# Attention in pairs of units and a values product of eight rounds, in a kernel of attention and two MLPs on one Trainium2 core

## The chip, the cores and the metric

The kernel runs on one core of one Trainium2 chip. The metric is device time in microseconds (us), the median of several executions. The engines are named as in the profile: PE (TensorE matmuls) and PEld (its weight loads), DVE (VectorE), ACT (ScalarE), POOL (GpSimd), SP (SyncE, which issues all the transfers here).

## The reference: what is computed

Attention with windows over 4 batches, 8 heads, 576 positions and 64 dimensions, then two MLPs on its 2304 x 512 output, all in float32:

```python
rel = pos[:, None] - pos[None, :]
mask_plain = (rel >= 0) & (rel < window)                                   # window 32, heads 0 to 3
mask_dil = (rel >= 0) & (rel < window * dilation) & (rel % dilation == 0)  # dilation 4, heads 4 to 7
scores = np.where(masks[None], scale * q @ k.T, -1e9)
attn = np.exp(scores - scores.max(-1)) ; attn = attn / (attn.sum(-1) + 1e-09)
x = (attn @ v)                       # as (2304, 512)
h = x @ w_in;  x = (h * sigmoid(1.702 * h)) @ w_out         # first MLP, 512 -> 2048 -> 512
h = x @ w_in2; y = relu(h) ** 2 @ w_out2                    # second MLP
```

## The kernel before

**Attention.** The dilated heads are reordered by the host so that both kinds of mask become a band: a query looks at its own block of 32 keys and the one before. A *unit* is one batch, one pair of heads and one half of the positions (288): 32 units in all, 8 a batch. For a unit `attend` (L488) loads q and k as one tile `qk` and three pieces of `v` (L497, L503), makes the scores of three blocks of 96 queries in 18 small matmuls on tiles of 64 rows by 32 columns of the array (`scores`, L517), adds the mask and takes the maximum on DVE (`maxima`, L530), exponentiates with a sum on ACT (`exps`, L537), adds 1e-9 and takes the reciprocal on DVE (L551, L554), normalises on POOL, ACT or DVE (L562), transposes in blocks of 32 on DVE (L575) and multiplies by v (`values`, L589). The values product goes block of queries by block: for each 32 queries, once with the keys before and once with their own keys, on three row groups and two column groups, 36 matmuls in all. Every matmul of float32 leaves two records in the trace, so a scores product shows as x36 and a values product as x72. Each is one round after another over the six array tiles. The results in PSUM are cast to a high part and a low part of x (L284 or L286 and L605).

**The MLPs.** They work on high and low parts, three matmuls for one product. The first MLP goes over five blocks of columns of x (`BLOCKS1`) and in each over 16 slices f of the hidden layer: `hidden` (L639 to L641, 12 matmuls), tanh on ACT, products on DVE, and `project` (L694 to L696, 12 matmuls). Its weights come as 64-bit words by L350 into three `raw` buffers, are put together by ACT or DVE (`raw_top`), DVE (`raw_join`, L361) and split into `wp` tiles, one for each two slices. The second MLP (from L1088) is by Strassen-like products. Attention of batch 0 comes first, ahead of the first block; the units of batches 1 to 3 are put in between the matmuls of blocks 0 to 2.

**The order.** `Schedule` (L100) is a planner that runs while the program is built: each task has a cost on its engine, a wanted time, the tasks it comes after and the buffers it takes, and the planner fixes the order of each engine from them. The constants at the head of the file (T_START, SCORES, SPACE and so on) are its costs and due times. While PE has nothing to do in the start, it puts warming matmuls on zeros in (L770). At run time every engine and SP's queue take their work in that order.

**Buffers.** Two `qk` and two `v`, three `sm`, two `pt` for every batch, so the load for a unit waits until a unit two earlier has been used. In PSUM there are three pairs of banks ("pr"; a unit's scores take one, its values one) and two single banks ("h"), of which the values of a unit take one and the hidden layer the others.

Of the kernel before, what the change touches and what calls it, by code (L numbers as in the profile page):

```python
# [7 lines left out]
F32 = mybir.dt.float32  # L8
# [28 lines left out]
T_START = 25.81  # L37
T_ATT = 2.38
A0 = 0.29
A1 = 0.82  # L40
SM_BUFS = 3
SCORES, VALUES = 0.74, 0.76
MAXIMUM, EXP = 0.13, 0.33

AHEAD = (47, 38, 43)
# [6 lines left out]
PREP = 9.31  # L52
# [3 lines left out]
RAW_FROM = 7.67  # L56
WARM = 256
WARM_FOR = 5
MASK_AT = -9.0
MASK_MORE = 10.0  # L60
LEAD = (23.0, 2, 5.33)
SPACE = 2.8
# [3 lines left out]
SPARE_POOL = (0.38, 2.22, 3.74)  # L66
SPARE_ACT = (0.54, 0, 0)
SPARE_TO = (33.64, 233.24)
# [10 lines left out]
UNITS = (8, 8, 8)  # L79
# [15 lines left out]
X_EARLY = 14.7  # L95
X_FROM = 3.48
X_WANT = 6.8
# [141 lines left out]
def attention_mlp_mlp(  # L239
# [27 lines left out]
    mask_sb = att.tile([QB, 5, P], BF16, name="mask_sb")  # L267
    mask_band = att.tile([QB, 5, 2 * WIN], BF16, name="mask_band")

    places = {  # L270
        "pr": 3, "o": 0, "h": 2, "s": 0, "c": C_BUFS, "qk": 2, "v": 2, "sm": SM_BUFS, "st": 3, "pt": 2,
# [150 lines left out]
    def x_pieces(b, p, u):  # L422
# [4 lines left out]
        per = size // NBLK  # L427
        jobs = []
        for n, blk in enumerate(BLOCKS1):
            width = sum(e - a for _, _, a, e in blk)  # L430
            runs, col = [], 0
            for bb, r, a, e in blk:
                if bb == b:
                    if plain:
                        lo, hi = max(a, size * u), min(e, size * (u + 1))
                        if lo < hi:
                            runs.append((r, lo - size * u, hi - size * u, col + lo - a))
                    elif r // 2 == u:
                        runs.append((0, (r % 2) * ROW + a, (r % 2) * ROW + e, col))
                col += e - a  # L440
# [3 lines left out]
            for r, lo, hi, c in runs:  # L444
                while lo < hi:
                    k = lo // per
                    end = min(hi, per * (2 if k == 0 and lo == 0 and hi >= 2 * per else k + 1))
                    cuts.append((r, lo, end, c))
                    c, lo = c + end - lo, end
            while cuts:  # L450
                r, lo, hi, c = cuts.pop(0)
                rows = 1
                inset = (lo + size * u) % ROW
# [9 lines left out]
                def src(m, r=r, rows=rows, lo=lo - k * per, hi=hi - k * per, k=k, both=both):  # L463
                    o = m["ab"][:, :, 0:QB] if both else m["c"][:, 0:QB] if k == 2 else m["ab"][:, k, 0:QB]
# [23 lines left out]
    def attend(b, p, u, want, start, n0):  # L488

        m = {}  # L490
        kinds = ((1, 0, 0), (0, 0, 0))[u] if p < NPAIR // 2 else (2, 3, 4)
        src = qkv_in[b, p, u]
        qk_b, v_b, sm_b, st_b, pt_b, s_b, ab_b, c_b = (buffer(c) for c in ("qk", "v", "sm", "st", "pt", "pr", "pr", "h"))

        def load_qk():
            m["qk"] = qkv.tile([P, UQ + UK], F32, tag="qk", bufs=2, name="qk")
            nc.sync.dma_start(m["qk"], src[:, 0:UQ + UK])  # L497

        def load_v():
            m["v"] = qkv.tile([QB, NBLK + 1, P], F32, tag="v", bufs=2, name="v")  # L500
            for a in range(NBLK):
                at = UQ + UK + a * P
                nc.sync.dma_start(  # L503
                    m["v"][a * WIN:(a + 1) * WIN], src[:, at:at + P].rearrange("(t k) d -> k t d", t=NBLK + 1)
                )

        d_qk = task("dma", 0.87, want - 5, load_qk, (), [qk_b])
        d_v = task("dma", 0.65, want - 1, load_v, (), [v_b], count=3)

        def scores():  # L510
            m["s"] = bank_pair(s_b)
            for i in range(NBLK):
                for a in range(NBLK):
                    w = (NBLK * a + i) * WIN
                    for j in range(2):
                        js = slice(D * j, D * (j + 1))
                        T.matmul(  # L517
                            m["s"][a * WIN:(a + 1) * WIN, j, i * KW:(i + 1) * KW],
# [882 lines left out]
```

## Time and profile before

| what | value |
|---|---|
| median of 3 runs | 837.87 us (836.74 to 838.67) |
| the profiled execution, its own time | 835.73 us |
| its span, from the first to the last instruction | 834.0 us |
| PE busy / PEld busy | 821.1 us (98%) / 739.8 us (89%) |
| DVE / ACT / POOL busy | 570.9 (68%) / 411.8 (49%) / 10.7 us (1%) |
| mean granted clock of TensorE | 0.994 |
| DMA | 171.70 MB, 206 GB/s over the span |

The profile is of one execution, whose time is 1.7 us more than its span. Busy shares are means over the whole span; the rows below look into single stretches. A start in a timeline is in us from the start of the span, and the second number is how long the group of instructions lasted; ends of matmuls are modelled, so starts are the safer numbers.

### The profile page before, as it was taken

How to read it: one execution, taken by the hardware profiler on the slowest of the kernel's cores; microseconds unless marked ns; L12 is line 12 of the kernel's file. 1: busy time of each engine (PE TensorE's matmuls, PEld its weight loads, DVE VectorE, ACT ScalarE, POOL GpSimd, SP SyncE). 2: the span in 40 equal slices, each digit the busy share in tenths (PEclk: the TensorE clock that was granted, in tenths of full speed). 3: DMA queues.
4: the chain of work that ended last, by engine and by line, in shares of the span. 5: the costliest groups of instructions: out<-in, count | busy, mean ns of one | idle time of the engine just before them, and what ended most of it. 6: DMA issues, size and time to landing. Idle time of an engine off the chain costs nothing.

```text
span 834.0 us, 18713 instructions
## 1 busy us (share of the span) xinstructions
PE 821.1 (98%) x7480; PEld 739.8 (89%) x7480; DVE 570.9 (68%) x1443; ACT 411.8 (49%) x1052; POOL 10.7 (1%) x23
## 2 busy tenths in 40 slices
PE   6999999999999999999999999999999999999998
PEld 4787778777789998888888899999999999999998
DVE  3788887645446778887797646587855687655784
ACT  5777676343336544443454345534455435455432
POOL 2200000000000000000000000000000000000000
PEclk9799999999999999999999999999999999999999
DMA  6666655221113248888956770877777696767751
GB/s 204 166 182 222 188 195 186 87 51 51 42 57 94 61 130 283 287 283 284 331 191 246 262 312 1 302 297 243 278 295 260 239 375 209 274 243 272 286 206 58
DMA packets 64311, 171.70 MB, mean 206 GB/s; under 512 B 6016, under 2 KB 36320, under 8 KB 58848
## 3 DMA queue, kind: packets, MB, share of 16 engines
q1 hardware_dynamic: 64224, 170.50, 59.4%
q8 instruction: 59, 0.97, 0.5%
q14 instruction: 28, 0.23, 0.1%
HBM read 131.68 MB, written 38.80 MB: 204 GB/s over the span
## 4 chain that ended last, share of the span: by engine, by line
PE 98%; issue 1%; DMA 1%; DVE 0%; ACT 0%; SPq 0%
PE ps L639 9%; PE ps L694 9%; PE ps L640 8%; PE ps L641 8%; PE ps L695 8%; PE ps L696 8%; PE ps L1244 7%; PE ps L1088 7%; PE ps L1089 7%; PE ps L1243 7%; PE ps L1245 7%; PE ps L1090 7%; PE ps L589 4%; PE ps L517 2%; PE ps L770 1%
## 5 line engine op out<-in xcount | busy, mean ns | idle before, releaser
L639 PE MATMUL ps<-x,wp 128*128 128x512 f32 (+3 forms) x328 | 123.1, 375 | 0.0
L694 PE MATMUL ps<-gh,wp 128*128 128x512 f32 (+3 forms) x328 | 122.2, 373 | 0.0
L640 PE MATMUL ps<-x,wp 128*128 128x512 f32 (+3 forms) x328 | 120.5, 367 | 0.0
L641 PE MATMUL ps<-x,wp 128*128 128x512 f32 (+3 forms) x328 | 120.4, 367 | 0.0
L695 PE MATMUL ps<-gh,wp 128*128 128x512 f32 (+3 forms) x328 | 119.3, 364 | 0.0
L696 PE MATMUL ps<-gl,wp 128*128 128x512 f32 (+3 forms) x328 | 119.3, 364 | 0.0
L1245 PE MATMUL ps<-gl,ws 128*128 128x384 f32 x336 | 112.2, 334 | 0.0
L1243 PE MATMUL ps<-gh,ws 128*128 128x384 f32 x336 | 112.2, 334 | 0.0
L1244 PE MATMUL ps<-gh,ws 128*128 128x384 f32 x336 | 112.2, 334 | 0.0
L284 ACT CAST gh<-gq 128x768 fp32r<-128x768 f32 x84 | 68.5, 838 | 78.3 <-PE ps L1244 57.5
L295 DVE TENSOR_TENSOR gl<-gq,gh 128x768 fp32r<-128x768 f32 x84 | 80.4, 957 | 34.2 <-PE ps L1245 28.2
L666 ACT ACTIVATE g<-ps 128x512 f32<-128x512 f32 (+3 forms) x82 | 44.7, 545 | 94.3 <-PE ps L641 94.0
L1088 PE MATMUL ps<-xo,ws 128*128 128x384 f32 x252 | 84.2, 334 | 0.0
L1089 PE MATMUL ps<-xo,ws 128*128 128x384 f32 x252 | 84.2, 334 | 0.0
L1090 PE MATMUL ps<-xo,ws 128*128 128x384 f32 x252 | 84.2, 334 | 0.0
L537 ACT ACTIVATE sm<-sm,st 96x64 f32<-96x64 f32 x192 | 64.5, 341 | 22.7 <-DVE st L530 22.4
L669 DVE SCALAR_TENSOR_TENSOR g<-g,ps 128x512 f32<-128x512 f32 (+3 forms) x82 | 50.5, 616 | 35.0 <-ACT g L666 34.5
L639 PEld LDWEIGHTS ps<-x,wp 128*128 128x128 f32 x328 | 62.8, 192 | 11.0 <-ACT sm L537 0.2
L641 PEld LDWEIGHTS ps<-x,wp 128*128 128x128 f32 x328 | 62.9, 192 | 10.0
L694 PEld LDWEIGHTS ps<-gh,wp 128*128 128x128 f32 x328 | 61.7, 188 | 11.1
L640 PEld LDWEIGHTS ps<-x,wp 128*128 128x128 f32 x328 | 63.0, 192 | 9.0
L696 PEld LDWEIGHTS ps<-gl,wp 128*128 128x128 f32 x328 | 61.8, 188 | 10.1
(73 smaller groups left out, 1427.4 us busy)
## 6 DMA issues: line engine op xcount, KB each, us to landing
ws<-wo_s SPq DMA_DIRECT2D x42, 1024.0 KB, 7.1
raw<-in_w SPq DMA_DIRECT2D x64, 511.8 KB, 4.7
ws<-wi_s SPq DMA_DIRECT2D x36, 896.0 KB, 6.4
wo_s<-wt SPq DMA_DIRECT2D x16, 896.0 KB, 7.5
wi_s<-wt SPq DMA_DIRECT2D x16, 896.0 KB, 6.0
qk<-in_qkv SPq DMA_DIRECT2D x32, 304.0 KB, 3.2
v<-in_qkv SPq DMA_DIRECT2D x96, 64.0 KB, 2.6
xs<-x2d SPq DMA_DIRECT2D x12, 384.0 KB, 5.8
```

The source lines that it names most:

```text
L639: T.matmul(out, w_hi[:, ks], x[:, 0, k, a:z], start=(k == 0), stop=False)
L640: T.matmul(out, w_hi[:, ks], x[:, 1, k, a:z], start=False, stop=False)
L641: T.matmul(out, w_lo[:, ks], x[:, 0, k, a:z], start=False, stop=(k == KD - 1))
L694: T.matmul(out, w_hi[:, ds_], m["gh"], start=(f == 0 and a == 0), stop=False)
L695: T.matmul(out, w_lo[:, ds_], m["gh"], start=False, stop=False)
L696: T.matmul(out, w_hi[:, ds_], m["gl"], start=False, stop=(f == KF - 1))
L1088: T.matmul(out, wt[:, 0, a, ks], hi, start=(first and k == 0), stop=False, skip_group_check=True)
L1089: T.matmul(out, wt[:, 0, a, ks], lo, start=False, stop=False, skip_group_check=True)
L1090: T.matmul(out, wt[:, 1, a, ks], hi, start=False, stop=(k == 1), skip_group_check=True)
L1243: T.matmul(out, w[:, 0, j, ds_], hi, start=(first and j == 0), stop=False, skip_group_check=True)
L1244: T.matmul(out, w[:, 1, j, ds_], hi, start=False, stop=False, skip_group_check=True)
L1245: T.matmul(out, w[:, 0, j, ds_], lo, start=False, stop=(j == NPR - 1), skip_group_check=True)
```

## The change

Three things, and new numbers for the planner.

1. Outside batch 0, `attend` takes both units of a head pair at once (`us = (0, 1)`): one scores product of 36 matmuls, twelve maxima and exponentials, one guard, one reciprocal, two normalisations, one transpose of 768 columns and one values product. `sm` and `pt` are single buffers of double width, `st` has four. Batch 0 still goes unit by unit.
2. The values product goes by keys. Each 32 keys of v are loaded into the array once, for the 64 queries that look at them (32 at both ends): 24 matmuls for a unit in place of 36.
3. In batch 0 q, k, v, sm, pt and the uncut masks lie in the places of the weight tiles 5, 6 and 7 of the first MLP, which are not in use then, so that no unit shares a buffer with another for q, k and v.

```diff
-T_START = 25.81
-T_ATT = 2.38
+T_START = 25.47
+T_ATT = 1.94
...
-SM_BUFS = 3
-SCORES, VALUES = 0.74, 0.76
+SM_BUFS = 1
+SCORES, VALUES = (0.74, 1.1), (0.8, 1.28)
...
-UNITS = (8, 8, 8)
+UNITS = (4, 4, 4)
...
+    first = {f: wpool.tile([P, 4096], F32, tag=f"wp{f}", bufs=1, name="first") for f in (5, 6, 7)}
+    q_first = [first[7][:, n * (UQ + UK):(n + 1) * (UQ + UK)] for n in range(6)]
+    q_first += [first[5][:, n * (UQ + UK):(n + 1) * (UQ + UK)] for n in range(2)]
+    v_first = first[6][:QB].rearrange("k (n t d) -> k n t d", n=8, t=NBLK + 1)
...
-    def attend(b, p, u, want, start, n0):
+    def attend(b, p, us, want, n0):
...
+        def load_qk(k):
+            m["qk", k] = q_first[n0] if first else qkv.tile([P, UQ + UK], F32, tag="qk", bufs=2, name="qk")
+            nc.sync.dma_start(m["qk", k], qkv_in[b, p, us[k], :, 0:UQ + UK])
...
-        scored = task("pe", SCORES, want, scores, [d_qk] + maxima_of.get(n0 - 2, []) + moved_of.get(n0 - SM_BUFS, []), [qk_b, s_b])
+        gate = maxima_of.get(n0 - 2, []) + moved_of.get(n0 - (4 if first else SM_BUFS), [])
+        scored = task("pe", SCORES[n - 1], want, scores, d_qk + gate, qk_bs + [s_b])
...
         def values():
-            m["ab"], m["c"] = bank_pair(ab_b), bank(c_b)
-            for i in range(NBLK):
-                for e in range(2):
+            ab, c = bank_pair(ab_b), bank(c_b)
+            for k in range(n):
+                ks = slice(QB * k, QB * (k + 1))
...
+                for i in range(NBLK + 1):
+                    lo, hi = max(0, i - 1), min(NBLK, i + 1)
                     for a in range(NBLK):
                         rows = slice(a * WIN, (a + 1) * WIN)
+                        o = (ab[:, a] if a < 2 else c)[:, ks]
                         for j in range(2):
                             js = slice(D * j, D * (j + 1))
-                            o = m["ab"][js, a] if a < 2 else m["c"][js]
                             T.matmul(
-                                o[:, i * WIN:(i + 1) * WIN], m["v"][rows, i + e, js], m["pt"][rows, j, i, e],
-                                start=(e == 0), stop=(e == 1), tile_position=(a * WIN, D * j), skip_group_check=True,
+                                o[js, lo * WIN:hi * WIN], m["v", k][rows, i, js],
+                                m["pt"][rows, k, j, max(0, i * KW - WIN):min(NBLK * KW, i * KW + WIN)],
+                                start=(i == 0), stop=(i == NBLK), tile_position=(a * WIN, D * j), skip_group_check=True,
                             )
...
-        for i, (p, u) in enumerate(ORDER):
-            attend(b, p, u, wants[(b - 1) * nu + i], False, b * nu + i)
+        for p in range(NPAIR):
+            attend(b, p, (0, 1), wants[(b - 1) * NPAIR + p], nu + (b - 1) * NPAIR + p)
```

What moves is shown at three places. The first is PE, just ahead of the first dense matmuls of the first MLP. Before (L517 scores, L589 values, L639 to L641 hidden layer):

```order
L589 MATMUL ps<-pt,v 64x32 x36
L517 MATMUL ps<-qk 32x64 x18
L589 MATMUL ps<-pt,v 64x32 x36
L517 MATMUL ps<-qk 32x64 x18
L639 MATMUL ps<-x_311,wp 128x288
L640 MATMUL ps<-x_311,wp 128x288
L641 MATMUL ps<-x_311,wp 128x288
```

And with the change (L623 values, L675 to L677 hidden layer):

```order
L623 MATMUL ps<-first 64x32 x6
L623 MATMUL ps<-first 64x64 x12
L623 MATMUL ps<-first 64x32 x12
L623 MATMUL ps<-first 64x64 x12
L623 MATMUL ps<-first 64x32 x6
L675 MATMUL ps<-x_326,wp 128x288
L676 MATMUL ps<-x_326,wp 128x288
L677 MATMUL ps<-x_326,wp 128x288
```

Ahead of the first dense matmul there are now the values of two units in one go, 24 matmuls each, and no scores of batch 1 any more. In both programs six units' values stand ahead of it and two behind. Warming matmuls are 28 in place of 40.

The second place is SP's queue in the start (L497 and L503 load q with k and v; L350 the first MLP's weights; L732 and L733 the later masks). Before:

```order
L497 DMA qk<-in_qkv 128x608
L732 DMA mask_sb<-in_masks 96x256
L733 DMA mask_sb<-in_masks 32x64
L497 DMA qk<-in_qkv 128x608
L503 DMA v<-in_qkv 32x4x128 x6
L497 DMA qk<-in_qkv 128x608 x2
L350 DMA raw<-in_w 128x2047 x3
L497 DMA qk<-in_qkv 128x608
L503 DMA v<-in_qkv 32x4x128 x3
```

With the change (L514 and L520 load q with k and v, L770 and L771 the later masks, L362 the weights):

```order
L514 DMA first<-in_qkv 128x608 x2
L520 DMA first<-in_qkv 32x4x128 x3
L770 DMA first<-in_masks 96x256
L771 DMA first<-in_masks 32x64
L514 DMA first<-in_qkv 128x608
L520 DMA first<-in_qkv 32x4x128 x3
L514 DMA first<-in_qkv 128x608
L520 DMA first<-in_qkv 32x4x128 x9
L362 DMA raw<-in_w 128x2047 x4
L514 DMA qk<-in_qkv 128x608 x2
L520 DMA v<-in_qkv 32x4x128 x6
```

The first three weight loads moved from behind 14 other transfers to behind 36, all of batch 0's loads among them.

The third place is PE in the first block of the first MLP, around a values product. Before:

```order
L639 MATMUL ps<-x_311,wp 128x512
L640 MATMUL ps<-x_311,wp 128x512
L641 MATMUL ps<-x_311,wp 128x512
L589 MATMUL ps<-pt,v 64x32 x36
L694 MATMUL ps<-gh,wp 128x512
L695 MATMUL ps<-gh,wp 128x512
L696 MATMUL ps<-gl,wp 128x512
```

With the change:

```order
L731 MATMUL ps<-gh,wp 128x224
L732 MATMUL ps<-gl,wp 128x224
L623 MATMUL ps<-pt,v 64x32 x6
L623 MATMUL ps<-pt,v 64x64 x12
L623 MATMUL ps<-pt,v 64x32 x12
L623 MATMUL ps<-pt,v 64x64 x12
L623 MATMUL ps<-pt,v 64x32 x6
L730 MATMUL ps<-gh,wp 128x224
L731 MATMUL ps<-gh,wp 128x224
L732 MATMUL ps<-gl,wp 128x224
```

One product of 48 matmuls for two units stands where two of 36 stood at different places. Batches 1 to 3 have 12 such products and 12 scores products of 36 matmuls, where there were 24 and 24 before. The dense matmuls of both MLPs are as many as before.

## Rows read from the trace of the kernel before

**Rows 1.** The page: busy time of each engine; chain that ended last, by engine.
```profile
PE 821.1 (98%) x7480; PEld 739.8 (89%) x7480; DVE 570.9 (68%) x1443; ACT 411.8 (49%) x1052; POOL 10.7 (1%) x23
...
PE 98%; issue 1%; DMA 1%; DVE 0%; ACT 0%; SPq 0%
```

**Rows 2.** Waits of PE, whole span: us in total, times, longest us.
```profile
PE ps L517 <- DMA qk<-in_qkv: 3.6, 2, 2.2
PE ps L517 <- issue: 2.7, 1, 2.7
PE ps L589 <- issue: 1.3, 1, 1.3
...
PE ps L589 <- DVE pt L575: 0.6, 2, 0.3
```

**Rows 3.** Timeline of PE, 30.4 to 35.7 us: start, us, engine, line.
```profile
31.35 0.69 PE L589 MATMUL ps<-pt,v 32*64 32x32 f32 x44 [0.30 <-DVE pt L575]
33.36 0.85 PE L589 MATMUL ps<-pt,v 32*64 32x32 f32 x28 [1.32 <-issue]
34.15 0.88 PE L517 MATMUL ps<-qk 64*32 64x64 f32 x36
34.96 0.61 PE L639 MATMUL ps<-x,wp 128*128 128x288 f32 x1
```

**Rows 4.** The page, DMA queues: packets, MB, share of 16 engines.
```profile
q8 instruction: 59, 0.97, 0.5%
```

**Rows 5.** Groups of ACT, 6 to 35 us: count, busy and mean ns, idle before.
```profile
L537 ACT ACTIVATE sm<-sm,st 96x64 f32<-96x64 f32 x44 | 14.8, 347 | 7.3 <-DVE st L530 7.3
...
L284 ACT CAST x<-ps 128x24 fp32r<-128x24 f32 (+7 forms) x22 | 3.3, 238 | 4.8 <-PE ps L589 4.8
L284 ACT CAST wp<-raw 128x512 fp32r<-128x512 f32 x3 | 1.8, 680 | 0.0
L284 ACT CAST c<-raw 128x512 f16<-128x512 bf16 x2 | 1.5, 760 | 0.0
```

**Rows 6.** Timeline of PE around a scores product, 77.2 to 79 us.
```profile
77.27 0.39 PE L694 MATMUL ps<-gh,wp 128*128 128x512 f32 x1
...
77.72 0.39 PE L696 MATMUL ps<-gl,wp 128*128 128x512 f32 x1
78.04 0.62 PE L517 MATMUL ps<-qk 64*32 64x64 f32 x36
...
78.94 0.40 PE L695 MATMUL ps<-gh,wp 128*128 128x512 f32 x1
```

**Rows 7.** Timeline of PE around a values product, 87.6 to 89.5 us.
```profile
87.85 0.39 PE L641 MATMUL ps<-x,wp 128*128 128x512 f32 x1
88.17 0.98 PE L589 MATMUL ps<-pt,v 32*64 32x32 f32 x72
...
89.41 0.39 PE L640 MATMUL ps<-x,wp 128*128 128x512 f32 x1
```

**Rows 8.** Stretches: us; busy PE, PEld, DVE, ACT, POOL; granted clock; DMA share; GB/s.
```profile
34.96:44.00 9.04, 9.04 (x184) 8.30 (x181) 5.35 (x30) 5.23 (x28) 0.83 (x1) 0.53 0.81 228
60.00:120.00 60.00, 60.00 (x764) 47.69 (x753) 52.56 (x171) 42.22 (x131) 0.00 (x0) 1.00 0.64 203
```

**Rows 9.** Timeline of SP's queue: start, us, line, transfers issued.
```profile
3.53 2.80 SPq L503 DMA_DIRECT2D v<-in_qkv  x6
...
8.73 1.38 SPq L350 DMA_DIRECT2D raw<-in_w  x3
...
12.96 2.37 SPq L503 DMA_DIRECT2D v<-in_qkv  x3
```

**Rows 10.** Line L350 (weights into raw), 0 to 45 us: issue to landing.
```profile
DMA to landing us min/median/max: 4.0/5.5/8.0
```

**Rows 11.** Groups of DVE by form: the low parts of the first MLP's weights.
```profile
L295 DVE TENSOR_TENSOR wp<-raw,wp 128x512 fp32r<-128x512 f32 x32 | 21.4, 677 | 0.2
```

**Rows 12.** Timeline of ACT: its first exponential.
```profile
6.05 0.35 ACT L537 ACTIVATE sm<-sm,st 96x64 f32<-96x64 f32 x1 [4.04 <-DVE st L530]
```

More of the change, by code (lines that the diff above doesn't have):

```diff
@@ L427, in x_pieces @@
         per = size // NBLK
+        before = size * u
         jobs = []
@@ L510, in scores @@
+        since = 0.0 if first else NEXT_FROM
+        d_qk = [task("dma", 0.87, at_qk, lambda k=k: load_qk(k), (), [qk_bs[k]], since=since) for k in range(n)]
+        d_v = [task("dma", 0.65, at_v, lambda k=k: load_v(k), (), [v_bs[k]], count=3, since=since) for k in range(n)]
         def scores():
-            m["s"] = bank_pair(s_b)
-            for i in range(NBLK):
[L513 to L518, printed above, removed]
-                            m["qk"][js, w:w + WIN], m["qk"][js, UQ + w:UQ + w + KW],
-                            start=True, stop=True, tile_position=(D * j, a * WIN), skip_group_check=True,
-                        )
@@ L523, in attend @@
-        scored = task("pe", SCORES, want, scores, [d_qk] + maxima_of.get(n0 - 2, []) + moved_of.get(n0 - SM_BUFS, []), [qk_b, s_b])
-        def maxima(j, i):
+            m["s"] = bank_pair(s_b)[:, :, 0:n * NBLK * KW].rearrange("q j (u c) -> q u j c", u=n)
+            for k in range(n):
+                for i in range(NBLK):
+                    for a in range(NBLK):
+                        w = (NBLK * a + i) * WIN
+                        for j in range(2):
+                            js = slice(D * j, D * (j + 1))
+                            T.matmul(
+                                m["s"][a * WIN:(a + 1) * WIN, k, j, i * KW:(i + 1) * KW],
+                                m["qk", k][js, w:w + WIN], m["qk", k][js, UQ + w:UQ + w + KW],
+                                start=True, stop=True, tile_position=(D * j, a * WIN), skip_group_check=True,
+                            )
@@ L577, in attend @@
-        moved = task("dve", 0.5, want, turn, [t], [sm_b, pt_b])
+                    out=sm, in0=sm, op=ALU.mult,
+                    in1=m["st"][:, 2, k].rearrange("q j (i o) -> q (j i) o", o=1).to_broadcast([QB, 2 * NBLK, KW]),
+                )
+        t = task("dve", 0.1, want, guard, es, [st_b], True)
+        t = task("dve", 0.15, want, recip, [t], [st_b], True)
+        ways = {"pool": 0.84, "dve": 0.44} if first else {"act": 1.5, "dve": 0.44}
+        normal = [
+            task(tuple(ways), tuple(ways.values()), want, lambda e, k=k: normalise(e, k), [t], [st_b, sm_b] + own, True)
+            for k in range(n)
+        ]
@@ L578, in attend @@
+        def turn():
+            m["pt"] = pt_first[:, pt_b["id"]] if first else att.tile([QB, n, 2, NBLK * KW], F32, tag="pt", bufs=1, name="pt")
+            V.transpose(
+                out=m["pt"].rearrange("k u j c -> k (u j c)"), in_=m["sm"].rearrange("q u j i c -> q (u j i c)")
+            )
+        moved = task("dve", 0.07 + 0.38 * n, want, turn, normal, [sm_b, pt_b] + own)
         moved_of[n0] = [moved]
         def values():
-            m["ab"], m["c"] = bank_pair(ab_b), bank(c_b)
@@ L644, in step @@
             if f < 2 and k == 0:
-                before = before + [v for u in range(2) if z > FIRST or u == 0 for v in values_of[blk["i"], u]]
+                before = before + [v for u in range(2) if z > FIRST or u == 0 for v in values_of.get((blk["i"], u), [])]
             t = task(
@@ L725, in attention_mlp_mlp @@
     nu = len(ORDER)
+    first_b = {f: buffer(f"wp{f}") for f in (5, 6, 7)}
     def load_masks():
```

190 lines of the change are left out of this document (98 added, 92 removed).

## The prediction

> **What bounds the kernel now.** I first read the busy shares and the chain that ended last [rows 1]: TensorE is busy for 98% of the span and is itself 98% of the chain. So only two things can shorten the run: fewer microseconds of work on PE, or less waiting on it. Next I read the waits of PE over the whole span [rows 2]. Apart from 1.1 us for the zeros of the first warming matmul there are four entries, 8.2 us in all, and none of them comes after the first layer has begun: from the first L639 on, PE waits for nobody. The timeline of PE at that place [rows 3] gives the start of the first layer, 34.96 us. I therefore split the profiled execution (span 834.0 us, time 835.73 us) into a start of 34.96 us, limited by latencies, and 799 us in which PE sets the pace, and reckon the two apart.
>
> The start is worth a closer look. Two of its waits, 2.73 and 1.32 us, have "issue" as their releaser and lie in the middle of a product (44 records of a values product, then nothing, then the other 28) [rows 2, 3]. No tile is waited for there. Queue q8 brought 59 packets [rows 4] for 14,960 instructions of PE and its loads [rows 1], some 254 to a packet, so I read these gaps as PE waiting for its own code. The other waits are for q and k (3.6 us). In the same stretch ACT, which does the exponentials, sat idle 7.3 us for DVE and 4.8 us for PE [rows 5], so no engine was full.
>
> After the start the cost of attention on PE is what it pushes the dense matmuls apart. Around a scores product [rows 6] the dense matmuls before and two after start at 77.72 and 78.94, 1.22 us apart; two steps of a dense 512-column matmul take 0.454 us (77.27 to 77.72 is two steps, 0.227 each), so the scores push in 0.77 us. Around a values product [rows 7] it is 87.85 to 89.41, 1.56 less 0.454, so 1.11 us. A scores product has 36 records in 6 rounds over its six array tiles, a values product 72 in 12. If a round costs the same in both, 6 rounds are 0.34 us: **0.057 us a round and 0.43 us fixed** for breaking into the dense stream.
>
> **The change, part by part, after the start.** (1) Values with each 32 keys once: 8 rounds a unit where there were 12. (2) Two units together: one fixed part where there were two, for scores and for values. Before, two units cost 2 x (0.77 + 1.11) = 3.75 us. Now the scores take 0.43 + 12 x 0.057 = 1.11 us and the values 0.43 + 16 x 0.057 = 1.33 us, so 2.44 us. That is 1.30 us for each of the 12 pairs of batches 1 to 3, 15.7 us. Two corrections: one scores product of batch 1 stood ahead of the first L639 before (34.15 in [rows 3]) and stands behind it now, +0.8 us; the two units of batch 0 still left behind it save 0.23 us each, -0.5 us. Together **-15.3 us**.
>
> The one unknown price is a round of 64 weight columns and 64 moving columns. The scores round has 32 and 64, the values round 64 and 32, and the trace has none with both wide. If the wider operand alone counts, a round stays at 0.057 us. If the sum of columns counts (96 in both old forms, 128 now), it is 0.076 us, and 4 such rounds in each of 26 units cost 2.0 us. I take 0.057, since the nearest rows, both with a 64 in them, give it, and keep 13.3 us of gain as the other end. No row gives less than 0.057.
>
> (3) On the other engines the exponentials, maxima and pieces of x stay as many; guard, reciprocal and transposes become fewer and longer. All this lies beside PE and is costed at nothing. The work that hides it is the dense stream, and the thinnest cover is 60 to 120 us, where DVE is busy 52.56 of 60 us and PE still never waits [rows 8]. With two to three pairs at 1.30 us less in it, the same DVE work has to fit into some 57 us, and DVE is 92% full. I allow **+0.5 us** for small new waits; where the cover goes altogether is a rival.
>
> **The start.** Batch 0's q, k and v now have places of their own, so no load waits for a buffer, but the first weights are issued behind all 36 transfers of attention and masks instead of behind 14. SP issued six in 2.80 us [rows 9], 0.467 each, so the first raw starts at 0.73 + 36 x 0.467 = 17.5 us instead of 8.73. Its transfer takes 4.0, 5.5 or 8.0 us (least, middle, most) [rows 10], so it lies there at 23.0 us in the middle case. Then ACT makes the top part (0.76), four exponentials and two casts that stand in between (1.3 and 0.3), the high part (0.68), and DVE the low part (0.68) [rows 5, 11]: 3.7 us, so 26.7 us. The join lies beside the exponentials. The other path is ACT's own: from its first exponential (6.05 [rows 12], unchanged, since the first masks and the first unit's q and k are still the first three issues) 42 exponentials of 0.336 (14.8 us for 44), 18 casts of 0.15 (3.3 us for 22), top and high part, together 18.3 us, so 24.3 us if it never waits [rows 5]; in-order waits, such as POOL cutting the later masks ahead of the third unit's normalisation, bring it near the first path. Both end close together. I take 28.0 us for the first dense matmul, between the middle and the slow transfer, because SP's pitch grew to 0.79 us (2.37 for three) while the DMA engines were loaded [rows 9]. Ends: 25.2 us with the quickest transfer, 30.5 with the slowest and a hand-over more. **34.96 - 28.0 = -7.0 us.** PE's code waits may come again, but a stop of PE now costs less: the next units' loads no longer wait for PE to free a buffer, so ACT and DVE have work queued meanwhile.
>
> At the start of the first layer the granted clock was 0.53 on average from 34.96 to 44 us [rows 8], near its lower level of 1.2 GHz, after the second code wait. The change keeps a stretch of this kind: fewer warming matmuls (28 for 40) and products between the first dense steps. I cost the difference at nothing, with -3 us (high level at once) and +2 us (a longer stretch) as ends.
>
> **Sum.** -15.3 + 0.5 - 7.0 = -21.8 us against 835.73, so **814 us**. The profiled execution stands 2.1 us under the median of the runs, 837.87, so by the median it would be 816; the range takes both in.
>
> **The rivals.** (a) *The wide round costs its sum of columns.* For it: each tile must take 64 weight columns and 64 moving ones. Against it: the two old rounds cost the same with either operand wide. Time 816. A rule of the Trainium skill would bring it about (page "TensorE: Matmul & The Clock Gate", section "Part 3: Packing small matmuls — row/col tiling"): a weight load overlaps a running matmul only in another row group, and here two tiles share each row group. No run here shows it for 64 by 64. Chance 0.15, next to the forecast and inside its range.
>
> (b) *The first layer waits for the weights.* If SP keeps the loaded pitch of 0.79 us [rows 9] for all 36, the raw starts at 29.2, lands at 34.7 and the first dense matmul is at 38.4: the start loses 3.4 us and 835.73 - 14.8 + 3.4 = 824 us. Against it: 0.79 was seen with three large weight loads in flight, which now come last. Chance 0.08.
>
> (c) *DVE and ACT become the bound in the first block.* For it: 88% of DVE in [rows 8], and single buffers for a pair's sm and pt, so that the next pair's scores wait for this pair's transpose. If the 5.2 us that four pairs save in this block are all waited away, 819 us. Chance 0.12.
>
> (d) *The pair's values hold their PSUM banks too long*, which ends on the other side. A pair takes a bank of "h" until both units' casts and subtractions are done, and the hidden layer has only two such banks; PE would then wait at each of the 12 pairs. It decides from 22 / 12 = 1.8 us of wait a pair; at 2.5 us it gives 814 + 30 = 844. Against it: with one unit's hold PE waited not once behind the start [rows 2], and the order leaves dense products of the second kind behind most pairs. Chance 0.04. That the change does less than it says is hardly open: the order shows 24 matmuls for a unit's values in place of 36.
>
> **How the numbers follow.** Forecast (808 to 818) 0.61, (a) 0.15, (c) 0.12, (b) 0.08, (d) 0.04. The range goes from 807 us (high clock at once and a start at 25.2, with all of the gain) to 823 us (waits of (c), or a late start, by the median's measure). A difference of 0.2%, 1.7 us, is about what a measurement of this kernel tells from none. Only (d), and (b) with (c) together beyond what each costs, end above that: slower 0.04, same 0.02, faster 0.94.
>
> **What would show it.** Right: the first dense matmul near 28 us; a pair's values with 96 records pushing in 1.33 us and its scores 1.11 us; no PE wait behind the start. A push of 1.49 us for the values would be (a); PE waits on DVE or ACT between 40 and 120 us (c); a first dense matmul after 33 us (b). The sum is wrong if PE still waits for code for several microseconds at the start, or if the stretch at the lower clock lasts beyond 15 us.

## The result and the profile after

| what | before | with the change |
|---|---|---|
| median of the runs | 837.38 us (836.74 to 838.67, 4 runs) | 815.66 us (815.59 to 816.05, 4 runs) |
| the profiled execution, its span | 835.73, 834.0 us | 815.61, 813.8 us |
| first dense matmul of the first MLP | 34.96 us | 30.81 us |
| from there to the end of the span | 799.0 us | 783.0 us |

The ratio is 0.974, with an interval of 0.972 to 0.976. The forecast was 814 us and a range of 807 to 823, so the time and the sign were right. Of 20.2 us of span, 4.15 came from the start and 16.05 from the part behind it; the forecast had 7.0 and 14.8. So the start brought 2.85 us less than forecast and the part behind it 1.25 us more. That the two partly cancel is luck; the rest of this document is about them.

The page of the changed kernel (busy times; chain that ended last, by engine), beside [rows 1]:

```profile
PE 800.2 (98%) x6700; PEld 727.0 (89%) x6700; DVE 556.1 (68%) x1380; ACT 420.2 (52%) x1074; POOL 10.3 (1%) x23
...
PE 96%; DMA 2%; SPq 1%; DVE 1%; ACT 0%; issue 0%
```

PE is still the bound, with 780 matmul records fewer (7480 to 6700). Its waits over the whole span (us in total, times, longest), beside [rows 2]:

```profile
PE ps L538 <- DMA first<-in_qkv: 4.5, 4, 2.1
PE ps L538 <- issue: 2.0, 2, 1.6
PE ps L623 <- DVE first L604: 1.8, 1, 1.8
...
PE ps L675 <- DVE x L641: 0.5, 1, 0.5
```

Only the last entry lies behind the start (it comes at 255.7 us). The stretch of the first block and that after the first dense matmul (columns as in [rows 8]):

```profile
34.96:44.00 9.04, 8.95 (x171) 8.35 (x172) 8.75 (x45) 7.14 (x27) 0.24 (x1) 1.00 0.85 276
60.00:120.00 60.00, 60.00 (x737) 48.79 (x736) 53.89 (x163) 47.44 (x156) 0.00 (x0) 1.00 0.71 217
```

DVE does 53.89 us of work in 60, more than before, and PE still never waits there: the thin cover held. From 34.96 to 44 us the granted clock is 1.00 (the level of 2.4 GHz) where it was 0.53. The clock records of this trace begin at 34.34 us; a row on a stretch ahead of that reads 1.00 for want of a record, so for the start the distance of equal dense steps has to serve instead.

The timeline of PE (start, us, engine, line): the end of the start, the first dense steps, the end of the first two slices, a pair's scores and a pair's values:

```profile
29.51 1.37 PE L623 MATMUL ps<-first 32*64 32x32 f32 x48 [1.75 <-DVE first L604]
30.81 0.61 PE L675 MATMUL ps<-x,wp 128*128 128x288 f32 x1
31.22 0.44 PE L676 MATMUL ps<-x,wp 128*128 128x288 f32 x1
31.46 0.44 PE L677 MATMUL ps<-x,wp 128*128 128x288 f32 x1
...
35.29 0.30 PE L676 MATMUL ps<-x,wp 128*128 128x288 f32 x1
35.42 0.29 PE L677 MATMUL ps<-x,wp 128*128 128x288 f32 x1
...
38.45 0.40 PE L730 MATMUL ps<-gh,wp 128*128 128x288 f32 x1
...
103.80 0.39 PE L732 MATMUL ps<-gl,wp 128*128 128x512 f32 x1
104.11 0.99 PE L538 MATMUL ps<-qk 64*32 64x64 f32 x72
...
105.38 0.39 PE L676 MATMUL ps<-x,wp 128*128 128x512 f32 x1
...
114.47 0.39 PE L732 MATMUL ps<-gl,wp 128*128 128x512 f32 x1
114.79 1.26 PE L623 MATMUL ps<-pt,v 32*64 32x32 f32 x96
...
116.31 0.39 PE L731 MATMUL ps<-gh,wp 128*128 128x512 f32 x1
```

Read as in [rows 6, 7], with two dense steps of 0.227 taken off: a pair's scores push 105.38 - 103.80 - 0.454 = 1.13 us (forecast 1.11), a pair's values 116.31 - 114.47 - 0.454 = 1.39 us (forecast 1.33). All seven products of each kind that stand between dense steps of 512 columns give the same push. The dense steps of 288 columns are 0.24 us apart at first and 0.13 from 35.29 on; in the kernel before all 24 of the first two slices were 0.24 apart, and its first step of `project` (L694) came at 44.42:

```profile
44.42 0.40 PE L694 MATMUL ps<-gh,wp 128*128 128x288 f32 x1
```

SP's queue in the start (columns as in [rows 9]):

```profile
4.49 1.38 SPq L520 DMA_DIRECT2D first<-in_qkv  x3
...
15.81 5.78 SPq L520 DMA_DIRECT2D first<-in_qkv  x9
21.64 8.74 SPq L362 DMA_DIRECT2D raw<-in_w  x4
```

What SP waited for up to 21.64 us (us in total, times, longest), and three links of the chain of waits there (start, us, what):

```profile
SPq L520 <- DMA first<-in_qkv: 2.2, 3, 1.0
...
SPq L514 <- DMA first<-in_qkv: 0.6, 1, 0.6
```

```profile
5.92 4.94 DMA first<-in_qkv
...
10.87 4.92 DMA first<-in_qkv
...
17.75 1.59 SPq L520
```

The pitch of SP is 0.47 us from the first transfer to the last wherever it does not stop. But it stops: 2.8 us in four waits for an earlier transfer to land, and some 1.5 us in two issues that took 1.59 and 0.78 us in place of 0.43. So the first weights are issued at 21.64 us, and over all 36 transfers the mean is (21.64 - 0.73) / 36 = 0.58 us. Each of the four waits ended when the transfer issued eight before had landed: the issue at 10.87 waited for the one of 5.92, and the one at 15.81 for the one of 10.87. From 5.92 to 15.81 us it is therefore eight landings of 4.9 us, and not SP's pitch, that set the pace, 0.62 us a transfer.

The chain of waits from 21.64 us to the first dense matmul (start, us, what; the rows left out are hand-overs, DVE's maxima and its parts of x):

```profile
21.64 4.49 DMA raw<-in_w
...
26.15 0.78 ACT c L296
...
26.96 0.86 DVE raw L373
...
28.97 0.49 DVE first L604
...
29.51 1.37 PE ps L623 x48
```

The weights' join (L373) stands in DVE's order ahead of maxima, parts of x and the transpose (L604) that the last values product ahead of the first layer needs. Late weights therefore hold up attention too.

### The profile page after: what moved, and what is told of

Read it like the earlier page. It is cut to its first block, busy times and chain, and to the rows that moved or that the text cites. A ratio compares the mean times of both kernels' runs of the same rounds, so it can differ in the third digit from the quotient of the medians.

```text
span 813.8 us, 17104 instructions
## 1 busy us (share of the span) xinstructions
PE 800.2 (98%) x6700; PEld 727.0 (89%) x6700; DVE 556.1 (68%) x1380; ACT 420.2 (52%) x1074; POOL 10.3 (1%) x23
## 4 chain that ended last, share of the span: by engine, by line
PE 96%; DMA 2%; SPq 1%; DVE 1%; ACT 0%; issue 0%
PE ps L675 9%; PE ps L730 8%; PE ps L677 8%; PE ps L676 8%; PE ps L732 8%; PE ps L731 8%; PE ps L1280 7%; PE ps L1125 7%; PE ps L1124 7%; PE ps L1278 7%; PE ps L1123 7%; PE ps L1279 7%; PE ps L623 2%; PE ps L538 1%; DMA first<-in_qkv 1%; SPq L520 1%
## 5 line engine op out<-in xcount | busy, mean ns | idle before, releaser
L675 PE MATMUL ps<-x,wp 128*128 128x512 f32 (+3 forms) x328 | 121.2, 370 | 0.7 <-DVE x L641 0.5
L677 PE MATMUL ps<-x,wp 128*128 128x512 f32 (+3 forms) x328 | 119.8, 365 | 0.0
L732 PE MATMUL ps<-gl,wp 128*128 128x512 f32 (+3 forms) x328 | 119.2, 363 | 0.0
L296 ACT CAST gh<-gq 128x768 fp32r<-128x768 f32 x84 | 68.7, 838 | 73.5 <-PE ps L1279 49.9
L675 PEld LDWEIGHTS ps<-x,wp 128*128 128x128 f32 x328 | 62.3, 190 | 11.1 <-DVE x L641 0.7
L677 PEld LDWEIGHTS ps<-x,wp 128*128 128x128 f32 x328 | 62.4, 190 | 9.8
L730 PEld LDWEIGHTS ps<-gh,wp 128*128 128x128 f32 x328 | 61.8, 188 | 10.4
L732 PEld LDWEIGHTS ps<-gl,wp 128*128 128x128 f32 x328 | 61.8, 188 | 9.8
L731 PEld LDWEIGHTS ps<-gh,wp 128*128 128x128 f32 x328 | 61.9, 189 | 9.5
```

What stands on the lines that cost most here:

```text
L675: T.matmul(out, w_hi[:, ks], x[:, 0, k, a:z], start=(k == 0), stop=False)
L677: T.matmul(out, w_lo[:, ks], x[:, 0, k, a:z], start=False, stop=(k == KD - 1))
L730: T.matmul(out, w_hi[:, ds_], m["gh"], start=(f == 0 and a == 0), stop=False)
L731: T.matmul(out, w_lo[:, ds_], m["gh"], start=False, stop=False)
L732: T.matmul(out, w_hi[:, ds_], m["gl"], start=False, stop=(f == KF - 1))
```

## The experiments

The theory after the result had four parts: a round costs the same in all forms; breaking into the dense stream has a fixed price; the new places shorten the start; late weights set its end. "Dense matmul" below is the first one of the first MLP, and every push is worked out as above.

**The parts taken away one at a time.** First, the values product of the changed kernel put back into its old form:

```diff
-                for i in range(NBLK + 1):
-                    lo, hi = max(0, i - 1), min(NBLK, i + 1)
-                    for a in range(NBLK):
...
+                for i in range(NBLK):
+                    for e in range(2):
+                        for a in range(NBLK):
...
+                                    start=(e == 0), stop=(e == 1), tile_position=(a * WIN, D * j), skip_group_check=True,
...
```

> The changed kernel, with the values product back in its old form (block of queries by block, 36 matmuls for a unit in place of 24), everything else and the order of every engine as in the changed kernel. Theory of rounds: a pair's values push the dense stream apart by 0.43 + 24 x 0.057 = 1.80 us instead of the 1.39 us measured with the change, so 12 pairs cost 4.9 us and the two units of batch 0 behind the start 0.2 us each: about 5 us above the changed kernel, 820.7 us, and the push of a values product of a pair reads about 1.8 us with 144 records. Rival, a round with 64 weight columns and 64 moving columns costs its sum of columns: the narrow rounds give back less, the difference is 3.2 us at most and the time 819 us. Rival, the values product by keys is worth nothing because the dense stream waits for something else there: no difference.

Measured 829.10 us (827.33 to 830.88, 6 runs), ratio to before 0.991 (0.988 to 0.993). Its timeline of PE:

```profile
40.41 0.98 PE L538 MATMUL ps<-qk 64*32 64x64 f32 x70
44.20 0.42 PE L538 MATMUL ps<-qk 64*32 64x64 f32 x2 [2.80 <-issue]
...
102.53 0.39 PE L732 MATMUL ps<-gl,wp 128*128 128x512 f32 x1
102.84 1.70 PE L623 MATMUL ps<-pt,v 32*64 32x32 f32 x144
...
104.81 0.40 PE L676 MATMUL ps<-x,wp 128*128 128x512 f32 x1
```

The push is 1.83 us for 24 rounds, as expected (1.80). But the whole is 13.4 us slower, not 5. In the profiled execution the dense matmul comes at 33.55 (2.7 us later), and PE stops for 2.80 us two records before the end of the first pair's scores. From 44 to 50 us it then runs at a granted clock of 0.50 (1.2 GHz), its 288-column steps 0.24 us apart again: some 5.6 us at about half the pace, so another 2.7 us or so. With 5.3 us for twelve pairs (12 x 0.44) and 0.2 for each of the two units of batch 0 that makes 13.9. The profiled execution (830.88 us) was the slowest of the six and stands 15.3 above that of the changed kernel; 1.4 us of this are not accounted for.

The same part alone, in the kernel before:

```diff
-            for i in range(NBLK):
-                for e in range(2):
-                    for a in range(NBLK):
...
+            for i in range(NBLK + 1):
+                lo, hi = max(0, i - 1), min(NBLK, i + 1)
+                for a in range(NBLK):
...
```

> The kernel before, with only the values product by keys (24 matmuls for a unit), no pairs and no other places for batch 0. Theory of rounds: 4 rounds fewer in each of the 26 units behind the start, 26 x 4 x 0.057 = 5.9 us less, 831.5 us; the push of a values product falls from 1.11 to 0.88 us; the start stays near 35 us. Rival, the wide round costs its sum of columns (0.076 us): 2.0 us less is gained, 833.5 us, push 0.96 us. Rival, 64 columns of weights and of moving data together cannot be had for the price of one: no gain.

Measured 824.17 us (823.71 to 824.96, 5 runs), 0.985 (0.983 to 0.987); the kernel before, run beside it, took 836.58, so 12.4 us less. Its timeline of PE:

```profile
29.83 0.40 PE L641 MATMUL ps<-x,wp 128*128 128x288 f32 x1
30.07 0.29 PE L642 MATMUL ps<-x,wp 128*128 128x288 f32 x1
30.20 0.29 PE L643 MATMUL ps<-x,wp 128*128 128x288 f32 x1
...
76.07 0.39 PE L643 MATMUL ps<-x,wp 128*128 128x512 f32 x1
76.39 0.77 PE L590 MATMUL ps<-pt,v 32*64 32x32 f32 x48
...
77.43 0.40 PE L697 MATMUL ps<-gh,wp 128*128 128x512 f32 x1
```

The push fell from 1.11 to 0.91 us (expected 0.88), 24 x 0.20 = 4.8 us in all. The start fell to 29.83, by 5.1 us, without any new place, and the first dense steps are 0.13 us apart from the second on. So part of what the prediction gave to the places belongs to the shorter values products: each takes 1.07 us in place of 1.45 at the slow pace of the start, and the second stop of [rows 3] did not come. The 24 steps at 0.13 in place of 0.24 save another 2.6 us. The three parts, 12.5 us, are about the 12.1 us between the spans of the two profiled executions.

The changed kernel without pairs in batches 1 to 3:

```diff
...
-        for p in range(NPAIR):
-            attend(b, p, (0, 1), wants[(b - 1) * NPAIR + p], nu + (b - 1) * NPAIR + p)
+        for i, (p, u) in enumerate(ORDER):
+            attend(b, p, (u,), wants[(b - 1) * nu + i], b * nu + i)
```

(The lines left out give `sm` three buffers and `pt` two again, and the planner the numbers for single units.)

> The changed kernel, but batches 1 to 3 unit by unit (three single buffers for the normalised scores, two for their transposes, as before); batch 0's places and the values product by keys stay. Theory of the fixed part: every pair is broken into two scores and two values products, 2 x (0.77 + 0.88) = 3.30 us against the 2.52 us measured with the change, so 12 pairs cost 9.3 us: about 825 us. Rival, pairing is worth only what the number of small matmuls makes it, and their number does not change: no difference, 815.7 us. Rival, the single buffers of the pairs make PE or DVE wait somewhere that the profile does not show as a wait: the time falls below that of the changed kernel.

Measured 825.28 us (823.79 to 827.23, 6 runs), 0.987 (0.984 to 0.989): 9.6 us above the changed kernel, and its pushes are 0.76 and 0.91 us. The fixed price is real, and the rival that only the number of small matmuls counts is out. The end of its start, 29.27, is set by late weights: they are issued at 21.07, ACT's cast of them (L296) stands ahead of eight exponentials in ACT's order, and PE waits 4.8 us for the transpose behind those (waits of PE, and a link of the chain):

```profile
PE ps L623 <- DVE first L604: 5.4, 2, 4.8
```

```profile
25.49 1.42 ACT first L558 x8
```

The same, with the old values product as well (both diffs above, of the first and of this run), so that the places alone are left:

> The changed kernel without pairs and with the old values product: of the change only batch 0's places of its own, the load order that goes with them and the planner's numbers are left. Theory: the start ends at about 31 us instead of 34.96 (4 us) and the stretch of the first layer at the lower clock is shorter by about 2 us; nothing after that is gained: 837.4 - 6 = 831.5 us. Rival, the two units of batch 0 and the order of the first layer decide the start, not the places: start near 35 us and 836 to 838 us. With the run without pairs and the run with the old values product, it also tells whether the parts add up: 837.4 down to this one (places), from this one to the one without pairs (values by keys, some 6 us), from that one to the changed kernel (pairs, some 9 us).

Measured 834.30 us (831.57 to 836.64, 12 runs), 0.997 (0.996 to 0.999): 2.3 us under before, not 6. The dense matmul came at 31.76, but the first 24 dense steps were all 0.24 us apart, as before, so the expected gain in that stretch did not come. Late weights set the end of this start too: they are issued at 22.05, and PE waits 2.6 us for the transpose.

In this order the parts add up: places 836.6 to 834.3, values by keys to 825.3, pairs to 815.7. In another order they don't weigh the same: values by keys alone already give 824.2, and the places on top of them nothing that can be measured (in that run late weights set the end of the start, as shown above).

The last of the kind: the changed kernel with batch 0's q, k and v in the two shared buffers and the load order of the kernel before.

```diff
...
-            qk_bs, v_bs, own = [first_b[7 if n0 < 6 else 5]], [first_b[6]], [first_b[5]]
...
+        qk_bs, v_bs = [[buffer(c) for _ in us] for c in ("qk", "v")]
...
```

> The changed kernel, but q, k and v of batch 0 go through the two shared buffers, with the loads and the first weights in the order of the kernel before; pairs and the values product by keys stay. Theory from the first four runs: values by keys alone gave 824.2 us and values by keys with the new places 825.3 us, so the new places of q, k and v are worth nothing (the start got shorter because its values products did), and pairs on top give 9 to 10 us: 814.5 to 815.5 us, with the first dense matmul near 30 us. Rival, as the forecast had it: without the places the units' loads wait for buffers again and the start grows by 4 to 7 us, 820 to 822 us.

Measured 821.55 us (819.69 to 822.18, 4 runs), 0.981 (0.979 to 0.983): the rival's time. Its waits of PE:

```profile
PE ps L621 <- DMA v<-in_qkv: 2.9, 1, 2.9
...
PE ps L621 <- DVE pt L602: 1.7, 2, 1.3
```

PE waited 2.9 us for the last units' v, and the dense matmul came at 32.01; between 82 and 99 us it waited 2.4 us more for DVE. So with pairs the places are worth some 6 us, and without them nothing. That run's order of loads is also not quite that of the kernel before (the last v pieces stand behind two more weight loads), so how much is the buffers' and how much the order's stays open.

**The weights earlier.** Two runs gave the first weight loads an earlier wanted time (the second with `{(0, 0): -5.0, (1, 0): 1.0}`):

```diff
+RAW_AT = {(0, 0): -9.0, (1, 0): -8.9, (0, 1): -8.8}
...
-        t = task("dma", 1.456, want - LEAD[0], load, (), [raw_b], since=RAW_FROM)
+        at = RAW_AT.get((f, part))
+        t = task("dma", 1.456, want - LEAD[0] if at is None else at, load, (), [raw_b], since=RAW_FROM if at is None else 0.0)
```

> The changed kernel with the first three weight loads put into SP's queue behind q and k of the seventh unit instead of behind all loads of attention. Theory: in the changed kernel the first weights were issued at 21.64 us and lay there at 26.13, and the join on DVE stood ahead of the maxima and transposes that the last values products waited for, so the first dense matmul came at 30.81; with the issue some 4 to 5 us earlier the wait of 1.75 us for that transpose goes and the first dense matmul comes at 28 to 29 us, 813 to 814 us in all. Rival: attention of batch 0 itself sets the start (its own loads, PE's products, the code waits), and early weights only take the DMA engines from it: first dense matmul at 30.8 us or later, 815 to 818 us.

> As the run with early weights, but the first weight load goes behind q and k of the eighth unit, the second between the last loads of v, the others last. Theory of late weights: half the gain, first dense matmul at 29 to 30 us, 814 to 815 us. Rival that attention sets the start: no difference, 815.7 us.

Both theories missed the time: 826.54 (825.56 to 828.13) and 825.81 us (824.42 to 828.18). The dense matmul came at 31.12 and 29.02, the second within what was expected. The main reason for the loss is neither weights nor attention. The planner had also changed orders far behind the start: ACT now took two copies of the first MLP's last results ahead of three short copies of the second MLP. PE waited for that, in the second run's timeline:

```profile
468.58 0.66 PE L1125 MATMUL ps<-xo,wt 128*128 128x384 f32 x1 [5.67 <-ACT ost L303]
```

(6.95 us in the other). The granted clock is 0.50 from 465.0 to 471.8 us there, so the first matmuls behind the wait go at half the pace, and the place costs 7.4 us (9.0 in the other) of the 9.4 and 11.1 between the spans of the profiled executions. The next runs therefore move only SP's queue; the orders of PE, DVE, ACT and POOL are those of the changed kernel:

```diff
+EARLY = {('v', 6): ('raw', 0, 0), ('v', 7): ('raw', 1, 0)}
...
-                t["fn"](e) if t["many"] else t["fn"]()
+                if t.get("key") in EARLY:
+                    early[EARLY[t["key"]]]["fn"]()
+                if t.get("key") not in EARLY.values():
+                    t["fn"](e) if t["many"] else t["fn"]()
...
```

The other two have `{('v', 7): ('raw', 0, 0)}` and `{('qk', 7): ('raw', 0, 0), ('v', 6): ('raw', 1, 0), ('v', 7): ('raw', 0, 1)}` for `EARLY`.

> The changed kernel with the first weight load moved in SP's queue ahead of the last but one load of v and the second ahead of the last one; the orders of PE, DVE, ACT and POOL stay word for word those of the changed kernel (the two earlier runs with early weights had also changed the planner's order behind the start, and lost 5.7 to 6.9 us to one wait for ACT in the second MLP). Theory of late weights: the join no longer holds up DVE, the first dense matmul comes at 29 to 29.5 us as in the run with weights between, and as nothing behind it has another order the gain stays: 814 to 814.5 us. Rival: the first block is paced by the chain of weight loads through three buffers, and an earlier start is given back there as waits of PE: 815.5 us. Rival on the other side: the two loads take the DMA engines from the last v pieces and the last values products come later: 817 us.

> As the run before it, but only the first weight load moves, by one place: ahead of the last load of v. Theory of late weights: some 1.7 us earlier for that load, half the gain, 815 us. Rival of the chain of weight loads: 815.7 us.

> As the two runs before it, with three weight loads moved: the first ahead of q and k of the last unit, the others ahead of the last two loads of v. Theory of late weights: 813.5 to 814.5 us. Rival that the loads of v suffer: first dense matmul at 31 us or later, 816 to 818 us.

| run | first weight issued | dense matmul | stops "issue" | median (lowest to highest, 5 runs) | ratio to before |
|---|---|---|---|---|---|
| changed kernel | 21.64 | 30.81 | 2.0 | 815.66 (815.59 to 816.05, 4 runs) | 0.974 (0.972 to 0.976) |
| two earlier | 17.03 | 30.70 | 3.1 | 815.18 (814.11 to 817.63) | 0.975 (0.973 to 0.978) |
| one earlier | 18.85 | 28.37 | 0.4 | 814.55 (813.63 to 816.63) | 0.974 (0.972 to 0.977) |
| three earlier | 15.54 | 29.40 | 1.5 | 814.95 (814.77 to 815.56) | 0.975 (0.973 to 0.977) |

Issue times, dense matmuls and stops are of one profiled execution each (816.62, 813.63 and 814.91 us for the three), and can be off by as much as the runs of one version differ. The loss of 10 us is gone with the old orders, so it lay in the planner's new ones and not in the early weights. But the gain from earlier weights is within what can be measured. In the chain of waits of the run with one load earlier the weights are still last (18.85 to 23.93), and its start is 2.44 us shorter (its first stop did not come either):

```profile
18.85 5.08 DMA raw<-in_w
...
23.95 0.78 ACT c L301
...
27.30 1.14 PE ps L631 x48
```

In the other two the chain runs through PE itself and its stops. So both theories hold in turn: late weights set the end of the start in the changed kernel, and once they are earlier, PE's own products and stops set it about as late.

**Without the warming matmuls.** One line, in the changed kernel and in the one with two weight loads earlier:

```diff
-        T.matmul(warm["o"][:, 0:WARM], warm["zeros"][:, 0:P], warm["zeros"], start=True, stop=True)
+        pass
```

> The changed kernel without its 28 warming matmuls on zeros, the order otherwise unchanged. [...] Without them small matmuls and dense steps stay at the slow pace for longer: start 1 to 2 us later and 1 to 3 us more in the first layer, 818 to 820 us. Rival: the warming matmuls only fill time in which PE would wait, and the pace depends on the dense matmuls alone: 815.7 us, or less by what the warming matmuls keep a product waiting.

> The first of these runs (two weight loads earlier) without the warming matmuls. Without them alone the start was 1.0 us shorter and had no stop in the middle of a product, the dense steps reached their quick pace at the same moment, and 2.4 us were lost between 60 and 120 us to waits for DVE, which itself waited for weights to land. If that was late weights, they are earlier now and the time is 813 to 815 us. If it is the chain of weight loads as such, 817 to 819 us again.

Measured 818.73 us (817.32 to 819.32, 4 runs), 0.978 (0.975 to 0.980), and 816.51 us (815.09 to 819.81, 5 runs), 0.977 (0.975 to 0.980). The expected slower start did not come: the dense matmuls are at 29.78 and 28.17, earlier than with the warming matmuls, and the quick pace begins at about 34 us in the first of them as in the changed kernel. In the first of them late weights set the end of the start again, through ACT as in the run without pairs (issued at 21.38; PE waits 4.2 us for the transpose), so this start could not show what warming is worth. What was lost lies between 60 and 120 us, as waits of PE for DVE (2.2 us in the first). DVE itself waited there, in the first run, from 60 to 100 us:

```profile
DVE raw L373 <- ACT c L296: 4.5, 3, 2.3
DVE c L298 <- DMA raw<-in_w: 1.4, 1, 1.4
```

In the second run, with weights earlier, 0.8 us of such waits were left, so weights that land late are the likelier cause; why they land later without warming matmuls stays open.

No version beats the changed kernel by more than the runs can tell; the one with one weight load earlier has the lowest median, 814.55 us.

## Why the prediction was right, and where it was not

- **The push of attention** was right in its mechanism and nearly in size. All forms that the runs show lie within 0.03 us of one line: scores of 6 and 12 rounds push 0.76 and 1.13 us, old values of 12 and 24 rounds 1.11 and 1.83, new values of 8 and 16 rounds 0.91 and 1.39. That line is 0.42 us fixed and 0.059 a round, where the prediction had 0.43 and 0.057. The prediction had taken it from two rows by assuming that a round of scores and a round of old values cost the same; by themselves the runs give 0.062 and 0.060, so the assumption held. A pair costs 1.13 + 1.39 = 2.52 in place of 2.44, twelve pairs save 14.8 in place of 15.7, and with the two corrections (+0.8, and 0.2 rather than 0.23 for each of two units) the term is -14.4, not -15.3.
- **Rival (a), the wide round at its sum of columns**, is out. New rounds, of which half are 64 by 64, cost (1.39 - 0.91) / 8 = 0.060 as the narrow ones do. The rule of the Trainium skill that was weighed there (page "TensorE: Matmul & The Clock Gate", section "Part 3: Packing small matmuls — row/col tiling") says which weight loads overlap a running matmul; no price for a wide round followed from it here.
- **The cover on DVE** held in the changed kernel, as forecast. The term of +0.5 us for new waits came out at 0.5, but at 255.7 us and not in the stretch that it was meant for, so its size is luck. With no other wait of PE behind the start, rivals (c) and (d) are out. That the cover is thin is shown by the runs that disturbed it: PE waits 2.2 us (without warming matmuls), 2.6 (old places) and 2.8 (weights between) from 60 to 120 us.
- **The start** was the term that failed: -4.15 in place of -7.0. Three steps were wrong. "SP issued six in 2.80 us, 0.467 each, so the first raw starts at 17.5": the pitch stayed, but SP stopped for 4.1 us in all, mostly for the transfer eight issues before to land, and it was 21.64. (The 0.79 that the prediction read as a loaded pitch in [rows 9] is three issues of which one took 1.52 us.) The landing then took 4.49 us, less than the 5.5 of the middle case, and the way from there to the dense matmul 4.7 in place of 3.7. So rival (b) had the right path, at about a third of its size (4.1 us of late issue, not 11.7). "The join lies beside the exponentials": it lies beside ACT's exponentials, but on DVE it stands in line ahead of the maxima and the transpose that PE waits for. And the gain was put down to the places, while values by keys alone, without places, brought 5.1 us.
- **The stretch at the slow pace** was costed at nothing, with -3 as one end. It was about -1.8 us: the first two slices with the products among them took 38.45 - 30.81 = 7.64 us in place of 44.42 - 34.96 = 9.46, and at the quick pace those products would push the same in both (0.91 + 0.91 + 1.13 and 1.11 + 1.11 + 0.76). Of it 1.3 us are 12 of the 24 dense steps at 0.13 instead of 0.24.
- **The code waits** came back, 1.61 and 0.43 us in place of 2.73 and 1.32. The prediction named them as what could spoil the sum, and read them as PE waiting for its code from a count of packets alone; the single packets bear it out (below). Whether and how long PE stops differs from run to run: from 0.2 us (without warming matmuls) to 4.4 (old values).

Against the profiled execution the terms found are -14.4 + 0.5 - 4.15 - 1.8 = -19.85, and the two executions differ by 20.1; 0.3 are left.

## What to carry to other kernels

Small tiled products that break into a stream of dense matmuls have a fixed price each (0.42 us here) beside the price of their rounds: put them together first, then make rounds fewer. A shorter program on the engine that sets the pace can be worth as much in the start as in the steady part (5.1 and 4.8 us for values by keys alone), in part since it moves or removes stops for code. Where a queue falls behind its pitch, look whether it issues slowly or waits for landings. And when an order comes from a planner, test a moved load with all other orders held fixed: here new wanted times for two or three loads cost 7 to 9 us more than four hundred microseconds later.

## What the runs showed of the hardware that was not expected

**PE stops at fixed places of its program.** The gaps with the releaser "issue" in the start come after the same few counts of records in all kernels, whatever stands there. The stretches up to the first and the second stop of the changed kernel (columns as in [rows 8]) are:

```profile
0.00:15.00 15.00, 8.74 (x222) 5.43 (x223) 5.85 (x61) 8.45 (x44) 3.69 (x11) 1.00 0.83 207
0.00:24.80 24.80, 17.31 (x476) 11.45 (x477) 12.13 (x118) 14.85 (x84) 7.54 (x20) 1.00 0.78 191
```

That is 445 and 953 records of PE and its weight loads. The kernel before stopped after 446 and 1464; the changed kernel with the old values product after 445, 955 and, for 2.80 us,

```profile
0.00:43.00 43.00, 31.43 (x986) 24.08 (x986) 26.18 (x174) 27.29 (x135) 10.65 (x23) 1.00 0.65 190
```

after 1972. The distances are some 508 to 510 records or twice that; one run also stopped after 699, half a distance further. Whether PE stops at such a place, and for how long (0.2 to 2.8 us), differs from kernel to kernel. What ends a stop is in the trace's records of single packets: queue q8 [rows 4] brings packets of 16 KB, and in the changed kernel such packets landed at 14.36 and 23.53 us and PE went on at 16.01 and 25.09. In all 24 gaps of this kind above 0.15 us, over all 14 traces, PE goes on 1.2 to 1.7 us after such a packet has landed. So PE waits there for its code. The Trainium skill (page "Runtime: NRT & Kernel Launch", section "Instruction fetch mechanics") says that instructions are refilled in blocks of 256, and calls the cost of a boundary "mostly hidden". The distances agree with two such blocks, and the 699 with one; that the cost is hidden does not hold in these starts, where the stops were 4.05 of 34.96 us before and 2.04 of 30.81 with the change.

**The quick pace can be lost behind a stop or a wait.** In two kernels a stop came while PE already ran at the quick pace, and the granted clock was 0.50 behind it: in the changed kernel with the old values product after the stop that ended at 44.20,

```profile
44.00:50.00 6.00, 5.80 (x26) 5.64 (x27) 1.73 (x19) 1.02 (x3) 0.00 (x0) 0.50 0.55 189
```

and in the kernel before after the stop of 1.32 us in [rows 3], as [rows 8] show. It need not be a stop for code: behind the wait of 2.9 us for v in the run with the old places the clock is 0.50 from 28.8 to 35.5 us, and around that of 5.67 us in the second MLP from 465.0 to 471.8. Nor does every stop do it: behind the one of 0.56 us at 36.12 in the last run without warming matmuls, and behind a wait of 1.42 us at 45.00 in the run with values by keys alone, it stayed at 1.00. The row alone does not tell every slow stretch: in the changed kernel the steps from 30.81 to 34 us were 0.24 us apart with a granted clock of 1.00 in the row, since its clock records begin at 34.34. The distance of equal dense steps is the surer reading.
